# Clearing the padded buffers of a zipformer block early on VectorE, with a new instruction order

## The chip, the cores and the metric

The kernel runs on one core of one Trainium2 chip. The metric is the device time of one execution in microseconds (us). The engines are named as in the profile: PE is TensorE (PEld its weight loads), ACT is ScalarE, DVE is VectorE, POOL is GpSimd, and SP is SyncE, which here only issues DMAs.

## The reference

One block of a conformer-like speech encoder on x of shape (2, 4000, 144), in bfloat16, with 4 heads of 36:

```python
x = x + 0.5 * (silu(layernorm(x) @ w_ff1a) @ w_ff1b)
q, k, v = split(layernorm(x) @ w_qkv)              # 4 heads, Dh = 36
x = x + (softmax(q @ k.T * Dh**-0.5) @ v) @ w_o    # over all 4000 keys
a, b = halves(layernorm(x) @ w_pw1)
c = depthwise_conv5(a * sigmoid(b), dw)            # along time
x = x + silu(c) @ w_pw2
x = x + 0.5 * (silu(layernorm(x) @ w_ff2a) @ w_ff2b)
out = layernorm(x)
```

## The kernel before

**Work.** The 8000 rows are cut into 16 chunks of 500, eight for each of the two sequences; a chunk is four blocks of 125 rows. For each chunk `pre` does the first feed-forward part and the projections to Q, K and V; attention then goes over key tiles of 64 rows, four heads at a time; `post1` does the output projection and the gated unit, `post2` the convolution, the second feed-forward part and the last layer norm. Keys of a whole sequence must be there before its attention can end, so the first eight chunks go through `pre` in a set-up stage of some 70 us, in which the first attention tiles already run. All other chunks' work is mixed into the attention.

**Softmax.** TensorE writes a pair of score tiles to two PSUM banks. For most tiles ScalarE takes the exponential of 1000 columns in one instruction (PT from PS, 128x1000). For 190 tiles VectorE computes it with bit operations. TensorE then multiplies PT with V (VA).

**Layer norm and transposition.** `ln` (line 1068) takes statistics on VectorE (ST), the reciprocal root on GpSimd (RS), and the normalised rows XN, on VectorE for the first three chunks and in the tail, otherwise on GpSimd. The rows must then be transposed. In the calm case TensorE does that. Otherwise `blocks` (line 994) transposes 32x32 blocks in XN on VectorE, writes them in four DMAs to a DRAM scratch (`rows`), and reads them back with two DMAs as XT or XTQ, all on the SP queue, in order. The attention output AN goes the same way.

**The buffers that are cleared.** XN has 5 buffers of 640 columns, of which 576 hold data; AN has 4 of the same shape; XT has 5 buffers, whose second part (80 rows, 512 columns) holds 16 rows of data, while matmuls read all 80. The rest must be zero once, and so each buffer is cleared before its first use. All these clearings are GpSimd instructions: XN in `ln`, first 64 columns and later the whole buffer, XT in `transp` (line 1038), AN in `setup_dw` (line 930).

```python
op("pool", "memset", XNS[:, u, :] if inter else XNS[:, u, n * D:n * D + 64], 0.0, w=[("XN", u)], cost=0.56)
op("pool", "memset", XT[0:LP, s, 1, :, :], 0.0, w=wk, cost=0.5)
op("pool", "memset", ANS[:, :, :], 0.0, w=[("AN", a) for a in range(NAN)], cost=2.2)
```

**What sets the order.** A planner (`Sched` and the loop at the end of the kernel function) runs the generators and records every operation with `Rec.op`, from modelled costs. Operations recorded between two steps on one engine form a block. Then `Rec.reorder` (line 279) moves the blocks of every engine by the distances that the table `ORDER` (line 38) spells, one character each, and `PLACES` (line 111) names the PSUM bank of every tile. Waits are derived afterwards from the reads and writes of the recorded operations. Every engine works through its list strictly in order. All recorded instructions have one line in the profile, that of `replay`.

Of the kernel before, what the change touches and what calls it, by code (L numbers as in the profile page):

```python
# [12 lines left out]
D = 144  # L13
# [5 lines left out]
LP = 80  # L19
# [3 lines left out]
NB = 4  # L23
# [21 lines left out]
        "OOPNQNQOYP]CNNNNOMPMSO[NKOOQNVMPMMN`NbYMMMMNOMNIcLLNL[MMMNNQNRMJQLLROQSPLRNOQOPUQOMPQMPPRPVPLQOMQNPQ"
        "QQQSKPQSQKQQQQJPPPPPWQQSPKKQQUPPPSWPQRPQAVPPPQCVPQRPWHSYPHSOPQYPQEPQCPRZUPPSOOHDPR^OKOOOOPNOOOO^NOQN"
        "NOOOSNNNNS[NNNdRMNRKYNJWJNNNNNNGOOPP^YNNNNOMNNNNRNNPPPVROOLOOPPRZNNOOOOOPNOSOPNRPSMOOPQOQWNRPRLLNSZP"
        "NPQOIOQOTPPPRPQ]P^USPMMQIQKQQ8QTQQGMRRTQQKRRRRGLRSOMRPQQQJQQRPVP[OOOQEROO^IOQLNOOPPTTOMNQ[FOQNPPSPPM"
        "HPQOQQUPLOPNVPNOOSQNLUOOPNOXPPPLTQNLMPPPQOPPTOOPTPLOOQRNOPPPQOVPNOOOORZOP[PPMOOFRZOL[ROQKQTUBOKNFPPP"
        "_OOOOOOPNOOOOWNNVNNXMNTKMNOMZQOSLNOMSPSLLTPMOOUOPNOOTQOMOPPPQOPPPQOPPPTTQOSQSSSSNEEPQOPTPTMOMORSNNOP"  # L50
        "ROYPQOPQ^NPNPQOPAOOOOOSOOOPPPQQNPPPPPPXOOOOOOOaNPPPLOOOPUMOOOO[IOOPSOOQNPHPSWOOPPPPQGPPPPQQQMPPQQNPQ"
        "O_OOOPZOOOPI_NNNNZOPEOQWP^HKPHSJOLNOO`VPMRJOM^J`MPNKUNLUGNLJQNRIOPPRXOMOOOOPXMOPPMOOOPWOOPPPTKNOOPPP"
        "PPPPPPPQRPSYSQNQYZPRRRADIOXQGVOPJOORPIPPRRSSMR]MHOOQQQVRKNHPLPPPPPPPPPPRZQSQRRbHSGNQGPPQRRGLPQKQQQQJ"
        "QOQRPMQOPPQOSQNRMTROTNPXQQQEPJOQNPRPN_OPPPLRSOPLPPPGPPPSeOMPPQRJZPKLNNNN`NOKOVJNNNNcM`LMMMNNN]MNL]LL"
        "LLLLTWLXKMMVNQ_LMOPPQQ>MOOOTOMRbMMOOOOOTOOOQZIOPJMOOcOMPPT[PRORPEVHOPYCJQOQQGMOQQNQWNQNPPLSP_OaOOOPN"
        "PDPPPLOHPPQLPPPPQOTPNWNPPPWJNPPP`OIOPPPPPPPUQOELRP^TTQOZUPPCGOPQDJPPPPPPRPQWPRURPMFQQ_RPXDPQJLPNOJPN"
        "PPPPPSPPQ`PPTQQRERPQIQTNDPTPPJOPQQNPPUOPPSLPMPPRPQQRPJP[RNQQLaRJQSS[IQMGQQRPCZJPQOPQTPP@RPIPPPPQQQSS"
        "VXUQGNTQSSETDS`OQSCJQQdLOINQMRLLZMNSMMMMZLWPK]JMNLMTLNNNNVN`NNNNNROOPPJQOPLRPRMOQQRPLPXQQQRPTUQHFPQJ"
        "PPPPPPSPROUSPPTLPUOCOPNQOPROTWPRWRPVRZOY^YEOOPPMQ:;QDQQQQQQQQQEQQQMQOROVSMOTTQLVHROTRGNTVPHRPTRaJSQE"
        "QRSKNRNOQOPWQO=OOPNYOOOQNNOO]QOL_PNRO^NOUIPNK_MMW>MMMZMMMM]MMQLMMSNNOMOPPSOVNNPNXNPQOKQOQLQQQQUPPPHO"  # L60
        "QORPQMQOPQQSQOUVWNWMNOKOAOQOPPPPZWNNNOOLNNR^MNVNOMNNNNPSMN]NTNNNNNaNNNOQLN[RNOMRNHMSOSNPQGPQOPRXRPQW"
        "KOHOPPQYPPZPQRCO[I^NORFNNIZMMMNOWLNNNQMNRORRO_KPNOOOYNNNNNNOU^NSUHNKOJNOSOOQRJUPROTYMHNNURNNTMIPNQOU"
        "OOV[MNLNNNPYTNeJLNORNNGOO[]NNNNIQLMRLNRWOPUOO]OM`QO;LSOLO]JOJPRLLMRUNZMOVR[NPDOT^OOOFOSTOMNOSbPQLPRS"
        "_MORR_NPP^OHCNNNOZOWL~NHLMMNNNSOOXNOQQNSSOIVKPNPN]NOOOOOPPVOOOITNPPLPPQOWPPMRPNTKOOTNOPUMOOOQN`OOOPN"
        "OOPPPLOZOQQMPIQO^YROQQRLENO_PNPPPTQNNOROOSVO]QMNRNOPWTNOMNSOPQXbOOOQ[NO~NCdIMMMMMMMfbKMMMQMMJLMPLMUM"
        "MMNL^TR^JSLJQJUKPNLHQMPP`UNNNNOMOOOOPNOOPPPPQQNPQQQMUQQMSOPTQOPTPQUNQSPSQ<TRSSVEQQQHQQFPPPPPQSPMYTOL"
        "NNTMNNNP^[NOMNNQMMOLNN]PNOOR[OPKQN_ZLNESMOOKHOM[NPPLPNOOPPMQSTMNPQQQQRSQRRTCQVNGRNOMTTTMMNUPPQHNQSPM"
        "YVTQKLLSSOIJPSSPTMKORNOQOPPPPPPSORNSMRNRRRNQQRPFRPQQQQQQRPFQO"
    ),
    "act": (  # L70
        "PPPPPPPPPPPPPRSNNOSOOOPPPPPPPUPNOXNNOOOOOQNPPPPPPPPPROOPPQOPPPQOPPPPPPQQNPPPPPPPPPPPPPPPPPPPPPPPPPQO"
        "PPPPPPPPPPPPPPPPPPPPPPPPPPPPPPPPPPPPPPPPPPPPPPPPPPPPPPPPPPPPPPPPPPPPPPPPQOROSNOOPPPPPPPPPPPPPPPPPPPP"
        "PPPPPPPPPPPPPQOPPPPPPPPPPPPPPPPPPPPPPPPPQOPPQOPPPPPPPPPPPPPPPPPPPPPPPPPPPPPPPPPPPPPPPPPPPPPPPPPPPPPP"
        "PPPPPPPPPPPPPPPPPPPPPPPPPPPPPPPPPPPPPPPPPPPPPPPPPPPPPPPPPPPPPPPPPPPPPPPPPPPPPPPPPPPPPQOPPPPPPPPPPPPP"
        "PPPPPPPPPPPPPPPPPPPPPPPPPPPPPPQOPPQOPPPPPPPPPPPPPPPPPPPPPPPPPPPPPPPPPPPPPPPPPPPPROOPPQOPPPPPPPPPPPPP"
        "PPPPPPPPPPPPPPPPPPQOPPPPPPPPPPPPPPPPPPPPPPPPPQOQOPPPPPPPPPPPPPPPPPPPPPPPPPPPPPPPPPPPPPPPPPPPPPPPPPPP"
        "PPPPPPPPTOPNOPPPPPPPPPPPPPPPPPPPPPPPPPPPPPPPPPPPPPPPPPPPPPPPPPPPPPPPPPPQOPPPPQOPPPPPPPPPPPPPPPPPPPPP"
        "PPPPPPPPPPPPPPPPPPPPPPPPPPPPPPPPPPPPPPPROOPPQQNPPPPPPPPPPPPPPPPPPQOPPPPPPPQOPPPPPPPPPPPPPPPPPPPPPPPP"
        "PPPPPQOPPPPPPPPPPPPPPPPPROOPPPPPPPPPPPPPPPPPQOPPPPPPPPPPPPQOPPPPPPPPPPPPPPPPPPPPPPPPPPPPPPPPPPPPPPPP"
        "PQOPPPPPPPPPPPPQOPPPPPPPPPPPPPPPPPPPPPPPPPPPPPPPPPPPPPPPPPPPPPPPPPPPPPPPPPPQOPPPPPPPPPPPPPPPPPPPPPPP"  # L80
        "PPPPPPPPPPPPPPPPPPPPPPPPPPPPPPPPPQOSPNRNOQOUQNPMOPPPRORNQNPPPPPPQOROQQMPPPPPPQOPPPWORNNNOO"
    ),
# [2023 lines left out]
```

## Time and profile before

| | before |
|---|---|
| time, median of 3 runs (lowest to highest) | 881.2 us (880.84 to 882.3) |
| the profiled execution: span from first to last instruction | 880.5 us |
| the span against the median | 0.7 us below |
| instructions | 27000 |
| granted TensorE clock, mean | 0.998 |

The time of the profiled execution is known by its span; the other times are of executions without a profile. Windows are counted in us from the start of the span. In a row of the timeline the columns are the start, the duration, the engine, the operation with its tiles, and in brackets how long the engine was idle before it and what ended that. In a row of the groups they are the busy time and the mean duration in ns, then the idle time before the group. In a row of the windows they are the window, its length, the busy time of PE, PEld, DVE, ACT and POOL with the number of instructions, the clock, the share of the DMA engines and GB/s. A row of the waits has the total, the number of times and the longest. In the chain of work that ended last each row is a start, a duration and the engine and tile that it followed.

### The profile page before, as it was taken

The page shows a single profiled execution, that of the slowest core. Times are in us where ns is not written, and L with a number is a line of the kernel's source. Part 1 is how long each engine was busy: PE and PEld are TensorE (multiplying, and loading weights), DVE is VectorE, ACT ScalarE, POOL GpSimd, SP SyncE. Part 2 cuts the span into 40 slices and gives each one's busy share as a digit, 9 for nine tenths or more (in the row PEclk, how much of TensorE's full clock was granted, in tenths as well). Part 3 has the DMA queues.
Part 4 walks back from the last instruction along what each step waited for, and adds up shares of the span by engine and source line. Part 5 has one row for each costly group of instructions (what it writes and reads, how often), then busy time and mean ns, then how long its engine had stood idle before and what let it go on. Part 6 is the DMA issues. An engine that isn't in the chain of part 4 may idle for free.

```text
span 880.5 us, 27000 instructions
## 1 busy us (share of the span) xinstructions
PE 851.5 (97%) x11419; PEld 380.2 (43%) x11419; DVE 822.7 (93%) x1812; ACT 849.6 (96%) x1098; POOL 300.4 (34%) x584
## 2 busy tenths in 40 slices
PE   8998999999999999999999999999999999999996
PEld 6543433344444443443444444344443433444366
DVE  7977999999999999999989999899999999999987
ACT  6799999999999999999999999999999999999986
POOL 7770331431336130252111813522513404032434
PEclk9999999999999999999999999999999999999999
DMA  3221001220221110212001120110110011001111
GB/s 100 44 55 38 16 18 36 62 51 16 40 49 38 23 38 22 45 24 45 16 9 30 36 44 23 23 26 20 43 31 18 21 37 20 17 12 36 27 27 33
DMA packets 114351, 28.80 MB, mean 33 GB/s; under 512 B 101090, under 2 KB 114230, under 8 KB 114230
## 3 DMA queue, kind: packets, MB, share of 16 engines
q1 hardware_dynamic: 112646, 26.39, 13.8%
q8 instruction: 89, 1.46, 0.7%
q10 hardware_dynamic: 1584, 0.69, 0.3%
q14 instruction: 32, 0.26, 0.1%
HBM read 13.44 MB, written 13.61 MB: 31 GB/s over the span
## 4 chain that ended last, share of the span: by engine, by line
ACT 46%; PE 33%; DVE 17%; POOL 2%; DMA 1%; issue 1%; SPq 1%; POOLq 0%; DVEq 0%
ACT PT L398 42%; PE PS L398 33%; DVE PT L398 7%; ACT TH L398 4%; DVE HT L398 2%; DVE ST L398 2%; DVE X L398 2%; DVE XN L398 2%; POOL RS L398 1%; POOL XN L398 1%; DVE KT L398 1%; DVE QT L398 1%; DVE AN L398 1%; SPq L398 1%; DMA rows<-XN 0%
## 5 line engine op out<-in xcount | busy, mean ns | idle before, releaser
L398 ACT ACTIVATE PT<-PS 128x1000 bf16<-128x1000 f32 (+1 forms) x818 | 757.2, 1074 | 4.1 <-PE PS L398 2.4
L398 PE MATMUL PS<-QT,KT 64*64 64x500 bf16 x3968 | 425.7, 385 | 13.0 <-ACT PT L398 5.2
L398 PE MATMUL PS<-PT,VA 64*37 64x500 bf16 x4728 | 411.5, 372 | 1.8 <-DVE QT L398 0.7
L398 DVE TENSOR_SCALAR PT<-PS 128x500 int16<-128x500 f32 x380 | 250.1, 668 | 5.8 <-PE PS L398 3.9
L398 PEld LDWEIGHTS PS<-QT,KT 64*64 64x64 bf16 x3968 | 123.4, 104 | 236.8 <-ACT PT L398 137.1
L398 POOL TENSOR_SCALAR RS<-ST 125x4 f32<-125x4 f32 x130 | 37.0, 284 | 482.2 <-DVE ST L398 475.6
L398 PEld LDWEIGHTS PS<-PT,VA 64*37 64x37 bf16 x4728 | 141.4, 96 | 96.2 <-DVE PT L398 18.7
L398 DVE TENSOR_SCALAR PT<-PT 128x1000 uint16<-128x1000 uint16 x380 | 154.5, 418 | 2.1 <-PE PS L398 0.8
L398 POOL TENSOR_SCALAR XN<-X,RS 125x144 bf16<-125x144 bf16 x260 | 150.4, 610 | 13.1 <-DMA out_dram<-XN 6.4
L398 DVE TENSOR_TENSOR PT<-PT 128x1000 bf16<-128x1000 bf16 x190 | 128.8, 679 | 1.3
L398 ACT ACTIVATE TH<-PS 128x500 bf16<-128x500 f32 (+3 forms) x194 | 107.3, 575 | 7.4 <-PE PS L398 6.5
L398 POOL TENSOR_TENSOR RS<-RS,NHALF 125x4 f32<-125x4 f32 (+1 forms) x93 | 91.7, 989 | 33.1 <-DVE RS L398 27.3
L398 DVE SCALAR_TENSOR_TENSOR HT<-TH,PS 128x500 bf16<-128x500 bf16 (+1 forms) x135 | 81.2, 615 | 12.8 <-ACT TH L398 12.0
L398 PE MATMUL PS<-XT,WA 80*128 80x500 bf16 (+5 forms) x288 | 74.5, 365 | 2.2 <-DMA XT<-rows 0.9
L398 DVE BATCH_NORM_STATS2 ST<-X 125x6 f32<-125x288 bf16 x160 | 65.7, 447 | 2.8 <-DMA X<-in_x_dram 2.7
L398 DVE SCALAR_TENSOR_TENSOR X<-PS,X 125x288 bf16<-125x288 f32 (+1 forms) x128 | 56.6, 449 | 6.5 <-PE PS L398 5.2
L398 PE MATMUL PS<-WB,HT 128*125 128x144 bf16 (+1 forms) x640 | 52.4, 230 | 0.7 <-ACT HT L398 0.5
L398 PEld LDWEIGHTS PS<-WB,HT 128*125 128x125 bf16 (+1 forms) x640 | 44.3, 136 | 14.5 <-issue 3.8
L398 PEld LDWEIGHTS PS<-XT,WA 128*128 128x128 bf16 (+1 forms) x288 | 21.2, 97 | 38.8 <-issue 10.6
L398 PE MATMUL PS<-U,DG 128*128 128x250 bf16 (+6 forms) x204 | 29.6, 264 | 0.0
L398 DVE STREAM_TRANSPOSE XN<-XN 128x320 f32<-128x320 f32 x54 | 27.0, 500 | 1.0 <-POOL XN L398 1.0
L398 POOL COPY U<-U 128x2 bf16<-128x2 bf16 (+1 forms) x54 | 9.2, 209 | 46.3 <-DVE U L398 46.3
(95 smaller groups left out, 522.6 us busy)
## 6 DMA issues: line engine op xcount, KB each, us to landing
rows<-XN SPq DMA_DIRECT2D x216, 40.0 KB, 2.0
XT<-rows SPq DMA_DIRECT2D x56, 128.0 KB, 2.0
rows<-AN SPq DMA_DIRECT2D x60, 40.0 KB, 2.0
X<-in_x_dram SPq DMA_DIRECT2D x15, 140.6 KB
XTQ<-rows SPq DMA_DIRECT2D x26, 70.3 KB
out_dram<-XN SPq DMA_DIRECT2D x13, 140.6 KB
XT<-rows SPq DMA_DIRECT2D x56, 16.0 KB, 1.9
out_dram<-XN SPq DMA_DIRECT2D x3, 70.3 KB
```

The source lines that it names most:

```text
L398: ins = getattr(eng, o.name)(*o.a, **o.k)
```

## The change

The clearings of XN, XT and AN are recorded at the start, as 14 instructions on VectorE: five whole XN buffers, five XT parts, four AN buffers. They take no time in the planner, and their step numbers (a fraction of 1) make each a block of its own, so that `ORDER` can put it where it likes. Where GpSimd's clearings were recorded, a "ghost" is recorded, which keeps the planner's course; `reorder` takes the ghosts out and hands what they waited for on to what waited for them. `ORDER` and `PLACES` are new throughout (not shown). No other operation is added or taken away.

```diff
     def reorder(self, table):
+        real = {}
+
+        def through(o):
+            if id(o) not in real:
+                ds = {}
+                for d, raw in o.deps:
+                    for x, how in through(d) if d.ghost else [(d, raw)]:
+                        if x is not o:
+                            ds[id(x)] = (x, how or ds.get(id(x), (x, None))[1])
+                real[id(o)] = list(ds.values())
+            return real[id(o)]
+
+        for o in self.ops:
+            drop = o.shared - o.own
+            o.deps = [(d, raw) for d, raw in o.deps if id(d) not in drop]
+        for o in self.ops:
+            if any(d.ghost for d, raw in o.deps):
+                o.deps = through(o)
+        self.ops = [o for o in self.ops if not o.ghost]
...
+    def side(like, *a, **k):
+        kept = dict(R.free), R.kind, R.last, R.filling
+        R.filling = True
+        o = op(*a, cost=0.0, **k)
+        R.free, R.kind, R.last, R.filling = kept
...
+        return o
+
+    def early(j, what, w):
+        side(None, "dve", "memset", what, 0.0, w=w).step = j / 64
+
+    for u in range(NXN):
+        early(1 + u, XNS[:, u, :], [("XN", u)])
+    for s in range(NXT):
+        early(11 + s, XT[0:LP, s, 1, :, :], [("XT", s, i) for i in range(NB)])
+    for a in range(NAN):
+        early(21 + a, ANS[:, a, :], [("AN", a)])
...
     def setup_dw():
-        op("pool", "memset", ANS[:, :, :], 0.0, w=[("AN", a) for a in range(NAN)], cost=2.2)
+        op("pool", "ghost", w=[("AN", a) for a in range(NAN)], cost=2.2)
...
-            op("pool", "memset", XT[0:LP, s, 1, :, :], 0.0, w=wk, cost=0.5)
+            op("pool", "ghost", w=wk, cost=0.5)
...
-            op("pool", "memset", XNS[:, u, :] if inter else XNS[:, u, n * D:n * D + 64], 0.0, w=[("XN", u)], cost=0.56)
+            op("pool", "ghost", w=[("XN", u)], cost=0.56)
...
-            op("pool", "memset", XNS[:, u, :], 0.0, w=[("XN", u)], cost=0.0)
+            op("pool", "ghost", w=[("XN", u)], cost=0.0)
```

More of the change, by code (lines that the diff above doesn't have):

```diff
@@ L45 @@
[L45 to L54, printed above, removed]
@@ new lines @@
+        "NLMQLNOPSHcKMMOIbMMMMr^LLLLMZ]LNNOIDKkCKOLJRVSJKSKINVJRMMZDL^NKNNKOXLPLY[KZQJTLIGTKKKMPVTQMNLNTQOXOK"
+        "OOOOPUMOOOOSYNNNPYPNPNIOYOOPSYNNNOXOaOOTOOIRP^KPNRPNLPRPNPTRVT]PU[WP!F]P]CFKHKMNNNNPQLRPVPSOJNNPROZP"
+        "MOQQMPPPJROSQTUVOKNOPEPTOOOYTObNOVQOM[DGQMSMPUMKNDOQT[MN[MMVMMOMKNRKQMaOOOOVNNNXMOMQJM]UQOPPUQOYPRAL"
+        "Q@PMOPPQQNPPQOPTO]NNNOOOSNNNN^NOOPNQOWZKPLM]OPHOORPN[D`NLMNNW_LLLOUKILLOR`NIPLQOYOPNPNGNN]MO]WMMMMMM"
+        "NLMXNTVNVJLLQTLQHTPLVO[LNNN]Q`KMKYLLUKLLMKNKZQM^MN[ULMNLILMTMMPSKOOQTPMROZLPPSLOMPPQKPRP^PLQQMVLQNPP"
@@ new lines @@
+        "JQJTPWOZPPPPJFOOOQ]PPQOIPPPUOOOPUPPQOWAYOOOOJXOPRPWHRYNG^OPPWOODPPEOPJYOOSPMMNOO[PNOOOPNOOOOQfNOSNNN"
+        "NORNUMMVYMMM`YGLPXHLYURLJKKLS?NOQOSQ[NLPPMOQNNROMPPPTPPPLPPPPS[NNNPNQNPM`NNOOPN^QMMMOMOOLPNPQUL^VXLM"
+        "KLQLPK]ZOMOOQRN[URNK]OQOCOO6OQNNO[OO[NNNOOOPJSOOJROQRPUKOOPNTTZMMMMY`MMMQMM_IMMNNSOOWKIPYMKRNKWMOMNO"
+        "PNSQUMMOPNTPNOORPNQUNOPNO^QOPLUSPLOLJOQUMOSNNNTOWNNPMUNNNORNXNOOOOOOWNORNOMUN[]MN^YNOMIN[NCKMOFUMNaM"
+        "MMXNNZMMQLLZKKZLLRKM[RLJLMTR^_KLLINU^LLLNKMZIMNQMMVPKMNOOPXO^NNOMNNNRPNe^NPPQRPICKOMNWNVKMMMURLJNOQO"
@@ new lines @@
+        "NPPPPPPPTOPNOPPPPPPPPPPPPPPPPPPPPPPPPPPPPPPPPPQOPPPPPPPPPPPQOPPPPPPPPPPQOPPPPQOPPPPPPPPPPPPPPPPPPPPP"
+        "PPPPPQOPPPPPPPPQOPPPPPPPPPPPPPPPPPPPPPQRNOPPQQNPPPPPPPQQNPPPPPPPPPPPPPPPPPPPPPPPPPPPPPPPPPPPQOPPPQOP"
+        "PPPQOQOPPPPPPPPPPPPPPPPPPPPPPPPPPPPPPPPPPPPPPPPPPPPPPPPPPPQOPQOPPPPPPPPPPQOPPPPPPPPPPPPPPPPPPPPPPPPQ"
+        "OPQOPPPPPPPPPPQOPPPPPPPPPPQOPPPPPPPPPPPPPPPPPPPPPQOPPPPPPPPPPPPPPPPPPPPPPPPQOPPPPPPPPPQQQMPPPPPPPPPP"
+        "PPPPPPPPPPPPPPPPPPPPPPPPPPPPPPPPPPPRROQLRTNNSNRMNPPPPPSORNNRPRMQQMRORPMPPPPPPQOPPPWORNNNOO"
@@ new lines @@
+    "0245042504250235042504250425042504250425042504235023502430342035301430245320542042052504240524053205"
+    "2405420524052450240524052504250425042505240524052405240552404202304104130453140314210412041204131043"
+    "1034015301330510351035153010351304024302430243014301430243023501530243034203422034320540130134021402"
+    "1402140214021402140214143134021402140214021401340204131041304120431043104031430154301240124240204134"
+    "0134021402140210421041204120412041203422043024302431043023502420340503134020412042104214124021402140"
@@ new lines @@
+    "2140214013401340214020412040214012041204120412140214021402140204120402141124021402045240240525042052"
+    "4035052405240240120402342034203530120412040214020412041204120412412412014013402143425301503510351341"
+    "0430420342035320340134013402140120430253015301530153015301301035023510340134031530130104301430243014"
+    "1430243024302430243024302351030324032402340234013410431340135301530153015031503513513104321340134031"
+    "0431410420411043104301430135013403104310412043134013401204120412041204120412040214021424302350342024"
@@ L130 @@
+    "2034203420342034205303240234034034302430234023402430234023402405320525032040254103512350240524052054"
+    "2405250425042020420552045205420524042404220534052042505240524053202505423042305220440342034203420341"
+    "0340143024203420243024202430243024034202340243203500351530240224033503510351035103510530153010413412"
+    "0412041201412042041204024012412140214021403140214042304143042136542300505465042125443120135545404221"
+    "354123415354102430106312"
 )
@@ L145 @@
 class Op:
-    __slots__ = ("eng", "name", "a", "k", "idx", "deps", "clock", "inc", "waits", "cnt", "q", "done", "t0", "t1", "kind", "step", "tile", "shared", "own", "acc", "base")
+    __slots__ = ("eng", "name", "a", "k", "idx", "deps", "clock", "inc", "waits", "cnt", "q", "done", "t0", "t1", "kind", "step", "tile", "shared", "own", "acc", "base", "ghost")
 class Place(int):
@@ L868, in bass_standalone__conformer_family_zipformer__speech_kernel @@
     op("pool", "memset", WK[:, :, :, :], 0.0, w=["WK0"], cost=0.3)
+    def side(like, *a, **k):
[3 more added lines that the diff above has]
+        R.free, R.kind, R.last, R.filling = kept
+        if like is not None:
+            o.done = like.done
+        return o
[7 more added lines that the diff above has]
+        early(21 + a, ANS[:, a, :], [("AN", a)])
     def setup_v():
```

121 lines of the change are left out of this document (51 added, 70 removed).

## The prediction, made before the changed kernel ran

> **What bounds the kernel now.** I read the page's totals first, then the busy time by stage, then the waits, and last the chain of work that ended last.
>
> ```profile
> span 880.5 us, 27000 instructions
> PE 851.5 (97%) x11419; PEld 380.2 (43%) x11419; DVE 822.7 (93%) x1812; ACT 849.6 (96%) x1098; POOL 300.4 (34%) x584
> ...
> 0.00:20.00 20.00, 17.05 (x201) 14.48 (x201) 13.90 (x58) 11.93 (x27) 13.66 (x39) 1.00 0.43 108
> 20.00:46.00 26.00, 23.45 (x240) 13.02 (x240) 25.02 (x64) 20.15 (x37) 20.79 (x42) 1.00 0.20 40
> 46.00:55.00 9.00, 8.83 (x130) 4.44 (x126) 5.88 (x15) 9.00 (x12) 6.79 (x16) 1.00 0.31 59
> 55.00:75.00 20.00, 18.06 (x240) 6.62 (x242) 12.29 (x24) 18.25 (x25) 6.88 (x11) 1.00 0.28 63
> 75.00:100.00 25.00, 24.39 (x356) 10.75 (x354) 24.11 (x49) 24.90 (x30) 5.62 (x11) 1.00 0.03 11
> 100.00:840.00 740.00, 725.83 (x9869) 304.54 (x9872) 708.46 (x1495) 736.09 (x905) 230.35 (x438) 1.00 0.14 30
> 840.00:880.50 40.50, 33.85 (x398) 26.31 (x390) 33.08 (x114) 29.31 (x68) 16.35 (x31) 0.96 0.10 27
> ```
>
> The stage rows give PE, PEld, DVE, ACT and POOL busy in that order. Over the whole span ScalarE lacks 880.5 - 849.6 = 30.9 us of being always busy, and its work (the softmax exponentials and the tanh steps) is the same before and after. So the change can win only what ScalarE now stands idle, plus what its instructions lose by not following one another closely. By stage that idle time is 8.1 us (0 to 20), 5.9 (20 to 46), 0 (46 to 55), 1.8 (55 to 75), 0.1 (75 to 100), 3.9 (100 to 840) and 11.2 (840 to the end). From 20 to 46 us VectorE is the full engine (25.02 of 26), and GpSimd has much to do (20.79 of 26); from 46 on ScalarE is full. GpSimd, which does the clearings, is a third busy on the whole, so relieving it can matter only in the first 75 us.
>
> **The change, part by part.** GpSimd loses sixteen instructions: the large clearing of AN, five full and five small ones of XN, five of XT.
>
> ```profile
> L398 POOL MEMSET XN<- 128x640 bf16 x5 | 3.2, 630 | 0.0
> L398 POOL MEMSET XT<- 80x512 bf16 x5 | 2.6, 519 | 0.0
> L398 POOL MEMSET AN<- 128x2560 bf16 x1 | 2.2, 2227 | 0.0
> ...
> L398 DVE MEMSET WA<- 80x256 uint32 x1 | 0.3, 272 | 0.8 <-PEq L2091 0.8
> ...
> L398 DVE MEMSET KL<- 128x128 uint32 x1 | 0.2, 165 | 0.0
> ```
>
> The first three rows make 3.2 + 2.6 + 2.2 = 8.0 us off GpSimd; the five small ones come on top. VectorE gets fourteen clearings that are issued as 32-bit words: five of 320 words (XN), five of 256 (XT), four of 320 (AN). The last two rows give (272 - 165) / 128 = 0.84 ns a word, so 320 words take about 0.33 us and 256 take 0.27 (row WA): 9 x 0.33 + 5 x 0.27 = 4.3 us on VectorE. The counts of all other work agree between the two programs.
>
> *Term 1, the first 20 us.* VectorE has holes there.
>
> ```profile
> 3.91 0.46 DVE L398 BATCH_NORM_STATS2 ST<-X 125x6 f32<-125x288 bf16 x1 [2.09 <-DMA X<-in_x_dram]
> ...
> 5.47 0.54 DVE L398 TENSOR_SCALAR XN<-X,ST,RS 125x144 bf16<-125x144 bf16 x2
> ...
> 6.83 0.54 PE L398 MATMUL PS<-IDENT,XN 125*128 125x125 bf16 x4
> ...
> 8.03 0.27 DVE L398 MEMSET VA<- 128x248 bf16 x1 [0.83 <-issue]
> ```
>
> In the new order seven clearings (four XN, three XT) and two old ones (WPZ, DG) stand ahead of the first statistics instruction: 4 x 0.33 + 3 x 0.27 = 2.1 us plus 0.36 for the old two (176 and 120 words). The hole for the first x load is 2.09 us, so the first statistics start up to 0.4 us late; but WPZ and DG used to stand between the first and the second, so the second is on time. One XN and one AN clearing, 0.66 us, follow in the chain to the first XN, which moves from 5.47 to about 6.1 and ends at 6.7. Its reader is the transposition at 6.83, behind the 50 warm-up matmuls: just covered. The other five (three AN, two XT), 1.5 us, stand around the VA group, against its hole of 0.83 us and smaller ones until 11 us. Without that cover all 4.3 us would go to the path; with all of it, none. I take **+0.1 us** (0 to +1.2), nearest the two large holes.
>
> *Term 2, 20 to 46 us.* Here GpSimd's clearings stand in line ahead of the layer-norm work that feeds the transposing DMAs.
>
> ```profile
> 15.88 0.81 DVE L398 BATCH_NORM_STATS2 ST<-X 125x6 f32<-125x288 bf16 x2
> ...
> 17.32 0.20 POOL L398 TENSOR_SCALAR RS<-ST 125x4 f32<-125x4 f32 x1
> ...
> 19.11 1.94 POOL L398 TENSOR_SCALAR XN<-X,RS 125x144 bf16<-125x144 bf16 x4
> ...
> 19.32 0.68 DVE L398 CAST VA<-PS 128x504 bf16<-128x504 f32 x1
> ...
> 27.07 0.83 SPq L398 DMA_DIRECT2D XT<-rows  x2
> ...
> 31.54 1.52 PE L398 MATMUL PS<-XT,WA 128*128 128x500 bf16 x6
> ...
> 35.02 1.49 PEld L398 LDWEIGHTS PS<-XT,WA 128*128 128x128 bf16 x8 [1.37 <-DMA XT<-rows]
> ...
> 35.46 3.66 DVE L398 SCALAR_TENSOR_TENSOR HT<-TH,PS 128x500 bf16<-128x500 bf16 x7
> ```
>
> Without them the first such layer norm starts when its statistics end (15.88 + 0.81 = 16.69) and not at 17.32; with 0.1 us for the hand-over it ends about 0.55 us sooner (20.5 instead of 19.11 + 1.94 = 21.05), the second 0.63 + 0.52 more, or 1.7 us, the third 2.9. The 1.37 us for which TensorE's weight loads wait for XT go. But what is late next is VectorE: the HT row shows seven evictions back to back, and VectorE has only 26 - 25.02 = 1.0 us left in this stage. So the cap is 1.0, not 1.37. The change also adds a wait: VectorE's first block transposition now stands right behind the eviction of VA, at 19.32 + 0.68 = 20.0 us, and waits for GpSimd until 20.5; behind it, in order, stand the XN, XT and HT steps and thus TensorE. That costs up to 0.5. On the SP queue the second chunk's four writes now stand ahead of the first chunk's two reads of XT, so these start about 27.6 instead of 27.07 (four writes behind a second transposition that GpSimd allows from about 24.5); TensorE uses them from 31.54 on, so that is covered. I take **-0.6 us** (-1.0 to +1.0).
>
> *Term 3, 55 to 100 us.* This is the place where GpSimd's lateness reaches ScalarE.
>
> ```profile
> 59.62 2.23 POOL L398 MEMSET AN<- 128x2560 bf16 x1
> ...
> 65.33 3.64 DMA rows<-XN
> ...
> 70.27 2.57 DMA XTQ<-rows
> 72.88 0.96 PE PS L398 x6
> ...
> ACT PT L398 <- PE PS L398: 0.9, 3, 0.6
> ACT TH L398 <- PE PS L398: 0.7, 1, 0.7
> ```
>
> The three rows of the chain in the middle say that the set-up's last transposing DMAs end last at 65 to 73 us, and the wait rows (total, times, longest) that ScalarE stands for 1.6 us behind them. These DMAs start when GpSimd has written XN; it gets there earlier by the clearings of XN and XT still ahead of it, and AN's 2.23 us are gone as well. The DMAs should come about 2 us sooner, more than the 1.6 that ScalarE waits. I take **-1.5 us** (-1.85 to 0, the stage's whole idle time).
>
> *Term 4, 100 to 840 us.* No clearing is left here; only the new order and the new bank numbers act. Counted in the two instruction streams, TensorE's instructions that wait for a semaphore fall from 1846 to 1749, by 5.3%; changes between attention and other matmuls fall from 803 to 794. TensorE stands 740 - 725.8 = 14.2 us in this stage: 5.3% of it is 0.75 us. ScalarE loses more than its 3.9 idle us:
>
> ```profile
> 735.70 0.96 ACT TH L398 x2
> ...
> 781.83 26.51 ACT PT L398 x30
> ...
> L398 ACT ACTIVATE PT<-PS 128x1000 bf16<-128x1000 f32 x740 | 690.9, 1085 | 3.0 <-PE PS L398 1.5
> L398 ACT ACTIVATE TH<-PS 128x500 bf16<-128x500 f32 x104 | 68.4, 673 | 0.0
> ```
>
> Where exponentials follow closely, one takes 26.51 / 30 = 0.884 us, and a tanh 0.48. 740 x 0.884 + 104 x 0.48 = 704, and the smaller forms about 15: some 719 of 740 us. The 21 us between are starts that TensorE was late for. 5.3% of 21 is 1.1. That waits can be weighed by their number is a choice, not a finding. I take **-1.0 us** between ends at +4 (the visible idle time doubles) and -7 (a third of the 21 recovered).
>
> *Term 5, the end.* The instructions behind the last exponential are the same but for one tanh and one eviction that swap sides, and VectorE is full there. I take **0** (-1 to +1).
>
> The sum is 0.1 - 0.6 - 1.5 - 1.0 + 0 = -3.0 us, so a span of 877.5. The profiled span of 880.5 is 0.7 below the median of the runs shown, 881.2, so the predicted time is 877.5 + 0.7 = **878.2 us**.
>
> [...]
>
> **The rivals.**
>
> *No change that can be measured* (a measurement of this kernel tells about 0.2%, 1.8 us, from none): VectorE, not GpSimd, paces the set-up. For it: 25.02 of 26 us. Against it: the chain through the transposing DMAs at 65 us. Terms 2 and 3 would shrink to 0 and -0.5, term 4 to 0: 880.5 + 0.1 - 0.5 + 0.7 = 880.8 us. Chance 0.15.
>
> *Slower: TensorE's in-order queue in the long middle.* Every block was moved, and a PT x VA group placed ahead of the next scores while its exponential isn't ready holds up those scores, and so ScalarE.
>
> ```profile
> PEld PS L398 <- ACT PT L398: 148.3, 406, 1.1
> ```
>
> The price of one such event is the mean wait, 148.3 / 406 = 0.37 us, when the two score pairs in PSUM no longer cover it. It decides from where these waits outlive the cover: the gains of terms 1 to 3 are 2.0 us, so six more uncovered events bring the time back and 11 make it slower by more than 1.8. With 15 such events in 740 exponentials: 880.5 - 2.0 + 5.6 + 0.7 = 884.8 us. Against it: fewer waits in the stream. Chance 0.15.
>
> *Slower: the early clearings hold GpSimd up.* Its set-up clearings run beside VectorE's, and the reciprocal root of the first layer norm stands behind them.
>
> ```profile
> 1.36 0.46 DVE L398 MEMSET WB<- 64x72 uint32 x3
> ...
> 1.46 0.21 POOL L398 MEMSET WO<- 80x144 bf16 x1
> ...
> 3.21 0.21 POOL L398 MEMSET WB<- 64x144 bf16 x1
> ```
>
> If they excluded each other, the seven new ones would push that root by 2.1 us and with it the set-up: 878.2 + 2.1 + 0.6 = 880.9 us (the gain of term 2 lost too). Against it: 144 columns took 0.21 us both beside VectorE's clearing and alone. Chance 0.03, in with no change.
>
> *Much faster: a tighter middle.* If the new order takes a third of the 21 us, 878.2 - 6.0 = 872.2 us; with a sixth, 875.7. For it: fewer waits. Against it: VectorE has only 740 - 708.5 = 31.5 us free there, so it can't absorb much. Chance 0.12.
>
> That the clearings aren't moved at all is excluded: the instruction streams show fourteen on VectorE and none of XN, XT or AN on GpSimd.
>
> **How the numbers follow.** Forecast 0.55, much faster 0.12, no change 0.15, clearings that hold GpSimd up 0.03 (880.9 is no change either), slower 0.15. The forecast's bounds reach over 879.4, the line of 0.2% under the median, so 0.07 of its 0.55 count as no change. Faster by over 0.2%: 0.48 + 0.12 = 0.60; within 0.2%: 0.07 + 0.15 + 0.03 = 0.25; slower: 0.15. The range runs from 874.5 (about 0.07 of the much faster case left out) to 883.6 (about 0.10 of the slower case left out), so that some 0.17 is outside. The forecast's own range is 876.0 to 880.0.
>
> **What would show it right or wrong.** Term 1: the first VectorE statistics at 3.9 to 4.4 us and the first transposition of XN on TensorE still at 6.8 to 7.0. Term 2: no wait for XT by TensorE's weight loads near 35 us, VectorE at 25.5 or more of the 26 us to 46, ScalarE idle there for about 5.3. Term 3: ScalarE waits under 0.4 us between 55 and 100 us. Term 4: ScalarE idle for about 3 us from 100 to 840, and the mean of the 1000-wide exponentials under 1085 ns. The prediction is wrong if ScalarE's idle time in the set-up stays near 16 us, or grows in the middle beyond 6.

## The result, and the profile after

The changed kernel takes **885.4 us** (median of 5 runs, 884.3 to 887.9) against 881.2 us (880.8 to 882.9): 1.0048 of the time before, 95% interval 1.0033 to 1.0064. It is slower by 4.2 us where I forecast 3.0 us less, and outside the range of 874.5 to 883.6. Measured a second time, beside later experiments, it took 884.7 us against 881.7 (1.0039, 1.0024 to 1.0055). The ratios with their intervals are estimates of their own and need not equal the quotient of the medians. One execution of a later run, e8, showed a mean granted clock of 0.848 and 924.7 us and is left out everywhere.

The profiled execution of the changed kernel is its slowest, 887.9 us with a span of 886.1; so its 5.6 us above the span of before overstate the median's 4.2. In every run the time is 1.8 to 1.9 us above the span. The profiled execution of before, span 880.5, is one of 882.3 us, 1.1 above its median. The prediction took 0.7 us from span to time; that amounts to taking its 3.0 us off the median (881.2 - 3.0 = 878.2), so no part of the miss comes from it.

First the totals, then the same stages as in the prediction (PE, PEld, DVE, ACT, POOL busy, then the clock):

```profile
span 886.1 us, 27034 instructions
PE 850.9 (96%) x11419; PEld 382.4 (43%) x11419; DVE 825.6 (93%) x1826; ACT 850.3 (96%) x1098; POOL 289.8 (33%) x568
```

```profile
0.00:20.00 20.00, 15.83 (x162) 13.72 (x163) 16.25 (x67) 9.77 (x22) 11.74 (x31) 0.91 0.43 109
20.00:46.00 26.00, 24.43 (x260) 13.20 (x257) 24.96 (x64) 22.41 (x42) 16.17 (x33) 1.00 0.18 39
...
55.00:75.00 20.00, 18.39 (x237) 7.07 (x237) 12.38 (x23) 18.45 (x25) 4.91 (x11) 1.00 0.27 61
...
100.00:840.00 740.00, 720.81 (x9852) 305.27 (x9846) 703.78 (x1489) 732.65 (x902) 227.56 (x437) 1.00 0.14 30
```

ScalarE does the same work (850.3 us). It now stands idle for 10.2 us up to 20 us (before 8.1), 3.6 from 20 to 46 (5.9), 1.6 from 55 to 75 (1.8), 7.4 from 100 to 840 (3.9), and 12.8 behind that (11.2). The set-up as a whole is where it was; in this execution the loss is in the long middle and behind it. The experiments will show that the set-up's total hides a gain and a loss. Three places stand out.

**The first 20 us.** VectorE's timeline of the changed kernel, the clearings around the VA group:

```profile
7.58 0.33 DVE L419 MEMSET AN<- 128x320 uint32 x1
...
9.01 0.27 DVE L419 MEMSET VA<- 128x248 bf16 x1 [0.82 <-issue]
...
9.75 0.27 DVE L419 MEMSET XT<- 80x256 uint32 x1
10.04 0.66 DVE L419 MEMSET AN<- 128x320 uint32 x2
...
11.38 0.27 DVE L419 MEMSET XT<- 80x256 uint32 x1
...
13.83 0.54 DVE L419 TENSOR_SCALAR XN<-X,ST,RS 125x144 bf16<-125x144 bf16 x2
```

The hole of 0.83 us ahead of the VA clearing, which I counted as cover, is still there with 0.82: it moved with the instruction behind it, from 8.03 to 9.01, and took nothing in. The XN that Q and K are made from comes at 13.83 instead of 13.00, as the timeline of before has it:

```profile
13.00 0.54 DVE L398 TENSOR_SCALAR XN<-X,ST,RS 125x144 bf16<-125x144 bf16 x2
```

TensorE's timeline of the changed kernel, and its windows, cut where the granted clock changed at 15.77 and 19.18 us, show what follows:

```profile
14.43 0.41 PE L419 MATMUL PS<-IDENT,XN 125*72 125x125 bf16 x4 [1.40 <-DVE XN L419]
...
15.50 0.39 PE L419 MATMUL PS<-IDENT,XN 125*128 125x125 bf16 x4 [0.49 <-DVE XN L419]
```

```profile
12.35:15.77 3.42, 1.53 (x25) 1.19 (x23) 3.35 (x15) 1.21 (x3) 2.20 (x4) 1.00 0.54 136
15.77:19.18 3.41, 3.41 (x26) 2.83 (x24) 2.78 (x11) 1.60 (x5) 2.18 (x5) 0.50 0.41 98
```

Behind two holes of 1.40 and 0.49 us the granted clock is 0.50, for 3.41 us.

**Near 185 us.** The SP queue, a step of the chain, and TensorE:

```profile
176.60 1.95 SPq L419 DMA_DIRECT2D XT<-rows  x2
178.59 0.70 SPq L419 DMA_DIRECT2D X<-in_x_dram  x2
179.33 2.56 SPq L419 DMA_DIRECT2D rows<-AN  x4
181.94 1.09 SPq L419 DMA_DIRECT2D XT<-rows  x2
```

```profile
182.61 3.60 DMA XT<-rows
```

```profile
186.26 0.89 PE L419 MATMUL PS<-XT,WP 128*128 128x500 bf16 x2 [2.10 <-DMA XT<-rows]
```

SP issues one DMA after the other, with 0.04 to 0.05 us between these rows. The read of XT that TensorE needs stands behind four writes of AN, starts at 181.94 and lands 3.60 us after its second part; TensorE stands for 2.10 us, and a half clock follows (0.57 in the mean from 186 to 190). In the order of before this read stood ahead of the writes of AN:

```profile
179.79 0.83 SPq L398 DMA_DIRECT2D XT<-rows  x2
180.67 0.32 SPq L398 DMA_DIRECT2D X<-in_x_dram  x1
181.03 2.56 SPq L398 DMA_DIRECT2D rows<-AN  x4
```

**The end.** The last row of the chain that ended last, before and after, and the queue's last issues in the changed kernel:

```profile
876.71 0.23 DVEq L2076
```

```profile
880.86 0.23 DVEq L2116
```

```profile
879.51 1.28 SPq L419 DMA_DIRECT2D out_dram<-XN  x3
```

VectorE's part ends at 881.09, 5.0 us ahead of the span's end; before it was 876.94, 3.6 us ahead. Three of the last output writes are issued within 1.3 us, as one that waits for ScalarE stands ahead of a large one.

### The profile page after: what moved, and what is told of

The parts are those of the page before. It is cut to its first block, busy times and chain, and to the rows that moved or that the text cites. A ratio compares the mean times of both kernels' runs of the same rounds, so it can differ in the third digit from the quotient of the medians.

```text
span 886.1 us, 27034 instructions
## 1 busy us (share of the span) xinstructions
PE 850.9 (96%) x11419; PEld 382.4 (43%) x11419; DVE 825.6 (93%) x1826; ACT 850.3 (96%) x1098; POOL 289.8 (33%) x568
## 4 chain that ended last, share of the span: by engine, by line
ACT 40%; PE 31%; DVE 22%; POOL 2%; SPq 1%; DMA 1%; issue 1%; POOLq 0%; DVEq 0%
ACT PT L419 36%; PE PS L419 31%; DVE PT L419 10%; ACT TH L419 4%; DVE HT L419 2%; DVE ST L419 2%; DVE XN L419 2%; DVE X L419 2%; SPq L419 1%; POOL RS L419 1%; POOL XN L419 1%; DVE AN L419 1%; DMA XT<-rows 1%; DVE QT L419 1%; DVE KT L419 1%
## 5 line engine op out<-in xcount | busy, mean ns | idle before, releaser
L419 PE MATMUL PS<-PT,VA 64*37 64x500 bf16 x4728 | 406.4, 372 | 0.4 <-DVE QT L419 0.2
L419 PEld LDWEIGHTS PS<-QT,KT 64*64 64x64 bf16 x3968 | 126.2, 104 | 244.8 <-ACT PT L419 132.7
L419 POOL TENSOR_SCALAR XN<-X,RS 125x144 bf16<-125x144 bf16 x260 | 145.8, 590 | 8.3
L419 ACT ACTIVATE TH<-PS 128x500 bf16<-128x500 f32 (+3 forms) x194 | 103.6, 549 | 8.9 <-PE PS L419 7.4
L419 PE MATMUL PS<-XT,WA 128*128 128x500 bf16 (+4 forms) x288 | 75.0, 364 | 3.6 <-DMA XT<-rows 1.5
```

Of the source, the lines that this page charges most:

```text
L419: ins = getattr(eng, o.name)(*o.a, **o.k)
```

## The experiments

**Theory Q**: the loss is made at two places of SP's queue, near 185 us and at the end. **Theory S**: it is made by the clearings around the VA group, which delay the set-up. **Rival M**: the new order loses a little in many places. Medians; "before" is the kernel before on the same chip in the same series.

| run | us | before | ratio (95%) |
|---|---|---|---|
| e1 old order, clearings on VectorE | 883.55 | 881.37 | 1.0021 (1.0012 to 1.0030) |
| e2 changed, first swap | 884.29 | 881.37 | 1.0032 (1.0019 to 1.0044) |
| e3 changed, both swaps | 883.54 | 881.37 | 1.0027 (1.0015 to 1.0038) |
| e4 new order, clearings on GpSimd | 882.88 | 881.37 | 1.0016 (1.0004 to 1.0028) |
| e5 e3, six clearings moved | 881.33 | 881.81 | 0.9997 (0.9988 to 1.0005) |
| e6 e4, both swaps | 880.99 | 881.81 | 0.9988 (0.9980 to 0.9997) |
| e7 e1, six clearings moved | 881.42 | 881.81 | 0.9999 (0.9990 to 1.0008) |
| e8 e3, more warm-up matmuls | 882.11 | 881.81 | 1.0008 (1.0000 to 1.0017) |
| e9 e5, all in holes, warm-up | 882.51 | 881.66 | 1.0008 (0.9999 to 1.0016) |
| e10 the changed kernel again | 884.74 | 881.66 | 1.0039 (1.0024 to 1.0055) |
| e11 e9 without more warm-up | 881.46 | 881.81 | 1.0003 (0.9995 to 1.0012) |
| e12 e5 again | 881.75 | 881.81 | 1.0001 (0.9992 to 1.0010) |

### e1 and e4: one half of the change each

e1, VectorE's list in the order of before (banks of before too):

```diff
 WA, WB clearings
+XN2 XT0 XT3 XT4 XN4 XN3 XN1
 ST (first), RS, WPZ, DG, ST (second)
+XN0
 RS
+AN3
 XN, XN (first chunk)
+AN2
 KL, VL, VA clearings
+XT2 AN0 AN1
...
 ST
+XT1
 ST
```

> The order of the blocks and the banks are those of the kernel before; only the fourteen clearings go to VectorE, at the neighbours that they have in the changed kernel. Theory Q (the time is lost at two places of SP's queue that the new order made, one near 185 us, one at the very end): no change, 881.2 us, between 880.3 and 882.1. Theory S (the five clearings around the VA group delay the set-up and let TensorE's clock fall, and that is not regained): 881.2 + 2.2 = 883.4 us. Both expect the first XN for the Q tile late by about 0.8 us and a granted TensorE clock of 0.5 somewhere between 15 and 20 us.

e4, the code of the changed kernel with the clearings recorded on GpSimd again:

```diff
-    for u in range(NXN):
-        early(1 + u, XNS[:, u, :], [("XN", u)])
...
-            op("pool", "ghost", w=wk, cost=0.5)
+            op("pool", "memset", XT[0:LP, s, 1, :, :], 0.0, w=wk, cost=0.5)
```

> The changed kernel's order and banks, with the clearings back on GpSimd as in the kernel before (the small ones at its start, the full ones ahead of their layer norms, AN with U ahead of the tap block). Theory Q: both places of SP's queue are still there, so 885.4 us (884.3 to 886.3). Theory S: without the clearings on VectorE the first 20 us are those of the kernel before, 885.4 - 2.2 = 883.2 us.

Both came out as theory S said, at 883.55 and 882.88: each half costs, 2.2 and 1.5 us, and together about what the change costs. Theory Q alone falls. In e1's profiled execution the XN for Q was late by 0.4 us, not 0.8 (13.42), and the half clock that both theories expected did not come (clock 1.00 up to 20 us): that execution took 882.9. The mean granted clock of every execution is on record, and in e1 it parts two groups: the four executions with 0.998 or 0.999 took 882.0 to 882.9 us, the seven with 0.996 or 0.997 took 883.5 to 884.4. That fits a delay that always costs and a clock that falls in some executions only. It is a sign and not a measure, as this mean also holds a half clock at the end of the span (3.0 us of it in before, 3.3 in the changed kernel).

### e2 and e3: two swaps in SP's queue

```diff
 XT<-rows x2, X<-in_x_dram x2
-rows<-AN x4
 XT<-rows x2, X<-in_x_dram
+rows<-AN x4
...
-out_dram<-XN 125x288
 out_dram<-XN 125x576
+out_dram<-XN 125x288
 out_dram<-XN 1x288
```

> The changed kernel with two neighbouring blocks of SP's queue swapped, so that the reads of XT that TensorE waits for at 186.26 us stand ahead of the four writes of AN and not behind them, as in the kernel before. Theory Q: the reads issue about 179.4 and land about 181.5, before TensorE asks for them at 184.2; the wait of 2.1 us, the half clock of 3.4 us behind it and ScalarE's 3.4 us go: 885.4 - 3.4 = 882.0 us (881.3 to 882.8). Rival M (the new order loses a little in many places, and this wait is an accident of one execution): 884.9 or more.

> As the kernel with the swap near 185 us, and a second swap in SP's queue at the end: the write of the output that waits for nothing new is issued ahead of the one that waits for ScalarE. Theory Q: from the last exponential to the end 36.5 us where the changed kernel had 38.0, so another 1.4 us: 882.0 - 1.4 = 880.6 us (879.7 to 881.5). Rival M: less than 0.4 us for this swap, as the last write, issued behind VectorE's last step, sets the end: 882.0 if the first swap does what theory Q says, 884.9 if not.

Against before of its own series the changed kernel is at +4.2 us, and +3.1 when measured again (e10); e2 is at +2.9 and e3 at +2.2. So the first swap brought 0.2 to 1.3 us where theory Q expected 3.4, the second 0.7 of 1.4. Neither theory's number was met, and the intervals of e2 and e3 overlap, so the second swap by itself isn't clear of noise. The mechanism is as expected; SP's queue and TensorE in e2:

```profile
179.05 0.83 SPq L419 DMA_DIRECT2D XT<-rows  x2
...
180.28 2.55 SPq L419 DMA_DIRECT2D rows<-AN  x4
```

```profile
183.91 0.61 PE L419 MATMUL PS<-XT,WP 128*128 128x500 bf16 x2
```

The read starts 2.9 us sooner and TensorE doesn't wait, though only just: by the trace's semaphores the read lands at 183.54, 4.1 us after its second part (theory Q: about 181.5). In the kernel before it took 1.8 us from there, in e3 4.1 and in e5 3.9, always ahead of the writes; so the 3.60 us in the changed kernel aren't the price of the four writes ahead, but the late start is. The size that theory Q expected was read from one execution, the slowest. At the end, e3:

```profile
878.45 0.23 DVEq L2116
```

From there (878.68) to the end of its span of 882.4 it is 3.7 us, as before the change, where the changed kernel had 5.0.

### e10: the changed kernel again

> The changed kernel itself once more, unaltered, beside the run with everything in holes. Theory Q with theory S: the wait for XT near 185 us is there in this execution too (TensorE idle there for 1.5 to 2.2 us), as is the late first XN for the Q tile (13.7 to 13.9 us), and the time is 885.4 us (884.3 to 886.4). Whether the granted clock falls behind the two holes may differ from execution to execution: with both falls about 887, with none about 884. Rival A (the wait at 185 us was an accident of one execution): no wait over 0.5 us there, and 883.0 or less.

884.7 us, as theories Q and S said. The XN for Q is late again (13.84) and the holes behind it are the same, 1.40 and 0.49 us, but the clock stayed at 1.00, and near 185 us the hole is smaller:

```profile
10.22:13.64 3.42, 2.63 (x39) 2.26 (x37) 3.37 (x14) 2.55 (x5) 0.53 (x1) 1.00 0.68 159
13.64:17.05 3.41, 2.12 (x26) 1.72 (x27) 3.30 (x15) 1.27 (x4) 2.94 (x6) 1.00 0.45 120
17.05:20.46 3.41, 3.41 (x56) 2.35 (x53) 3.27 (x10) 3.24 (x10) 2.65 (x6) 1.00 0.29 59
```

```profile
184.38 0.62 PE L419 MATMUL PS<-XT,WP 128*128 128x500 bf16 x2 [0.77 <-DVE PT L419]
```

The hole of 0.77 us misses the 1.5 to 2.2 that I had expected; TensorE's weight loads waited 1.2 us for XT there. The same read at the same place landed 2.3 us after its second part, not 3.60. The two executions of one kernel differ by 886.1 - 882.9 = 3.2 us and by two half clocks of 3.41 us, at which TensorE loses 3.41 x (1 - 0.50) = 1.7 us each at most, by my estimate.

### e5, e6, e7: what is left when the faults are taken out

Six clearings moved (e5 in the new order, e7 in the old):

```diff
 RS
-AN3
 XN, XN (first chunk)
-AN2
 KL, VL, VA clearings
-XT2 AN0 AN1
 ST, ST
-XT1
+XT2 XT1
 ST
...
 VA<-PS
+AN0 AN1 AN2 AN3
 QT<-PS
```

> The changed kernel with both swaps in SP's queue, and with the six clearings that stood between the first layer norm's steps and around the VA group moved: the four of AN into VectorE's hole of 2.23 us near 66 us, two of XT behind the two statistics that end at about 9.5 us, where VectorE waits for x. Theory S (what is left, 883.5 against 881.4, is the delay of the set-up that these clearings make, with the half clock of TensorE behind it): the first XN for the Q tile moves from 13.8 to about 13.0 us, no half clock before 20 us, 883.5 - 2.0 = 881.5 us (880.6 to 882.3). Rival R (the rest of the new order, or the seven clearings ahead of the first statistics, cost it): 883.5 (882.7 to 884.3).

> The changed kernel's order and banks with the clearings on GpSimd, now with both swaps in SP's queue. By the terms measured so far they add up: 882.9 - 1.1 (the swap near 185 us) - 0.75 (the swap at the end) = 881.0 us (880.2 to 881.9). Rival R (the rest of the new order is dear as well): 882.4 or more.

> The order and banks of the kernel before with the clearings on VectorE, the six moved as in the run with the changed order. Theory S: the 2.2 us that the clearings cost in this order go, 881.4 us (880.6 to 882.2), and nothing is won, as the set-up's end does not hang on GpSimd. Rival R (the seven clearings ahead of the first statistics cost it): 883.0 or more.

All three were met: 881.33, 880.99, 881.42. In e5's timeline of VectorE the XN for Q is back at 12.88:

```profile
9.33 0.82 DVE L419 BATCH_NORM_STATS2 ST<-X 125x6 f32<-125x288 bf16 x2
10.15 0.55 DVE L419 MEMSET XT<- 80x256 uint32 x2
...
12.88 0.55 DVE L419 TENSOR_SCALAR XN<-X,ST,RS 125x144 bf16<-125x144 bf16 x2
```

The stages of e5, and then of e6, whose clearings are on GpSimd:

```profile
0.00:20.00 20.00, 16.07 (x201) 13.18 (x201) 17.20 (x68) 11.84 (x27) 13.10 (x34) 1.00 0.43 109
20.00:46.00 26.00, 23.86 (x240) 13.13 (x244) 24.58 (x64) 21.90 (x39) 16.27 (x33) 1.00 0.21 43
...
55.00:75.00 20.00, 19.08 (x252) 6.77 (x250) 14.54 (x28) 19.20 (x26) 3.51 (x8) 1.00 0.27 68
...
100.00:840.00 740.00, 722.78 (x9900) 306.93 (x9896) 706.72 (x1496) 735.81 (x905) 227.81 (x437) 1.00 0.14 30
```

```profile
0.00:20.00 20.00, 16.71 (x213) 13.55 (x213) 14.40 (x58) 12.68 (x29) 14.39 (x42) 1.00 0.43 110
20.00:46.00 26.00, 23.98 (x248) 13.08 (x240) 24.71 (x64) 21.50 (x38) 18.86 (x39) 1.00 0.22 44
...
55.00:75.00 20.00, 18.94 (x252) 6.74 (x244) 13.10 (x24) 19.39 (x25) 6.04 (x9) 1.00 0.28 69
```

In these three stages of the set-up ScalarE's idle time is 8.2 + 4.1 + 0.8 = 13.1 us in e5, and 7.3 + 4.5 + 0.6 = 12.4 in e6, against 15.7 before. Other executions show less: 14.1 in e12 (e5's kernel again), 13.9 in e4, and e7, with the old order, has 14.5. So with the clearings on VectorE the new order wins 0.4 to 1.4 us of idle time there (e12 and e5 against e7), with the clearings on GpSimd 1.8 to 3.2 (e4 and e6 against before), each from single executions. In the middle both have 4.1 to 4.2 us (100 to 840 of e6: 735.87 us busy), like before (3.9). e6 is the only version whose interval leaves out 1 on the faster side, and just so; it beats before by 0.8 us in the median, less than the 0.2% that I set as readable. The pair e4 and e6 gives both swaps a second time: +1.5 and -0.8 against before, so 2.3 us, and here the intervals don't overlap.

### e8: the clock by itself

```diff
-FILLS = (5, 2, 5, 12, 3, 1, 3) + (0,) * 60
+FILLS = (5, 2, 5, 26, 6, 1, 3) + (0,) * 60
```

> The changed kernel with both swaps, the clearings where they are, and 17 more warm-up matmuls on TensorE (14 and 3, of 0.056 us each) in its two holes at 13.0 and 15.0 us, which shrink from 1.40 and 0.49 to about 0.62 and 0.32 us. Theory C (it is the half clock that costs, not the late first XN): the granted clock stays 1.00 from 12 to 20 us, the first exponential starts about 1.5 us sooner than in the changed kernel, at 20.3, and the time is 883.5 - 1.3 = 882.2 us (881.4 to 882.8). Rival D (the delay of 0.85 us costs, and the half clock is regained by 46 us in any case): 883.5 (882.9 to 884.2).

882.11 us: theory C. The clearings are at their costly place, the XN for Q is as late, but TensorE's holes are filled:

```profile
14.44 0.41 PE L419 MATMUL PS<-IDENT,XN 125*72 125x125 bf16 x4 [0.62 <-DVE XN L419]
```

e3 is the same kernel with the holes, e5 the one without the delay as well. Against before of their series they are at +2.2 (e3), +0.3 (e8) and -0.5 us (e5): 1.9 for the clock and 0.8 for the delay (by the plain medians 1.4 and 0.8). The intervals of e3 and e8 just meet and those of e8 and e5 overlap, so the split is less sure than the whole. ScalarE's first exponential of 1000 columns shows the same split in the traces of before, of e8, and of the changed kernel:

```profile
19.29 1.04 ACT L398 ACTIVATE PT<-PS 128x1000 bf16<-128x1000 f32 x1
```

```profile
20.33 1.00 ACT L419 ACTIVATE PT<-PS 128x1000 bf16<-128x1000 f32 x1 [0.17 <-PE PS L419]
```

```profile
21.74 1.00 ACT L419 ACTIVATE PT<-PS 128x1000 bf16<-128x1000 f32 x1 [0.17 <-PE PS L419]
```

The late XN moves it by 1.0 us, the half clock by another 1.4; in e10, whose clock didn't fall, it starts at 20.33 too. So where the clock falls, more than half of what the six clearings cost is the clock.

### e9, e11, e12: everything in holes

e9 leaves six clearings ahead of the first statistics, puts WPZ and DG behind them again, XT4 with XT1 and XT2, AN near 66 us, and sets the two counts of FILLS to 20 and 6; e11 sets them back to 12 and 3; e12 is e5 once more.

> The changed order with both swaps in SP's queue, all fourteen clearings on VectorE, now only in its holes: six ahead of the first statistics (WPZ and DG again between the first and the second), one XN behind them, three XT where VectorE waits for x near 9.5 us, four AN near 66 us; and 8 and 3 more warm-up matmuls in TensorE's two holes at 13 and 15 us. Theory S (a clearing costs what it delays the chain to the first XN for the Q tile, nothing more): first statistics at 3.9 us, that XN at 12.9 to 13.0, no half clock, and 0.3 us under the run with six clearings moved: 881.0 us, 0.998 to 1.000 of the kernel before. Rival R (on GpSimd they are cheaper in any case, as VectorE is full up to 46 us): 881.6 or more, above the kernel before.

> The run with all fourteen clearings in holes, without its 11 more warm-up matmuls. That run was at 882.5 us in the median although its profiled execution (881.0) showed all that theory S expects of it. Theory F (the added matmuls cost in executions that were not profiled): 881.2 us (880.5 to 881.8). Theory P (three XT clearings and WPZ and DG at their new places cost): 882.5 (881.9 to 883.1). Neither, if it and the repeat of the run with six clearings moved agree with each other within 0.5 us.

> The run with both swaps and six clearings moved, once more and unaltered: 881.3 us by its first measurement (880.8 to 881.8), and 3.4 us under the changed kernel. If it comes out at 882 or more, the differences of 1 us between runs of different calls are not to be read, the one of the run with everything in holes among them.

e9 missed: 882.51 instead of 881.0, in the range of rival R, though its profiled execution (881.0 us, XN for Q at 12.95, clock 1.00 from 12 to 17 us) is what theory S says. e11, 881.46, and e12, 881.75, agree within 0.3 us. So the places of the clearings in e9 don't cost, and e9's 1 us is left to its 11 more matmuls or to chance; the intervals of e9 and e11 overlap, and this stays open. Rival R itself isn't excluded: with the clearings on GpSimd e6 is at -0.8, with them on VectorE e5, e11 and e12 are at -0.5, -0.4 and -0.1, and the intervals overlap. e12 and e5 are one kernel, and the clock is where their profiled executions part; e12, cut where its clock changed:

```profile
19.96:23.37 3.41, 1.91 (x22) 0.73 (x22) 2.39 (x8) 3.27 (x5) 2.87 (x7) 1.00 0.07 14
23.37:26.79 3.42, 3.42 (x20) 1.12 (x17) 2.99 (x8) 2.56 (x3) 2.95 (x6) 0.50 0.25 44
```

From 23.37 to 26.79 us e12's clock is 0.50; in e5 it is 1.00 there, behind the same holes. e12's span is 880.3, e5's 879.0: one half clock of 3.4 us goes with 1.3 us of the whole in this pair. In another pair, e11 with a mean clock of 0.996 and e9 with 0.997, the spans are 879.7 and 879.1, 0.6 us apart. In e5 and e12 TensorE is idle for up to 1.6 us in a stretch of 3.41 us there, in the kernel before for 1.0 at most.

## Why the prediction was wrong

The result is 7.2 us above the forecast. 3.0 of them are the gain that I had forecast (terms 2 to 4) and that hardly reaches the time. The other 4.2 are losses that the sum didn't hold: the clearings of term 1 that had no cover, and the SP queue, near 185 us (in the stage of term 4) and at the end (term 5).

**Term 1 (+0.1, 0 to +1.2): failed.** The failing step is "The other five (three AN and two XT) ... stand around the VA group, against its hole of 0.83 us and smaller ones until 11 us", with the value taken "nearest the two large holes". That hole is "issue", time in which VectorE waited for nothing that the profile shows, and it moved with the VA clearing. The five stood on the chain to the XN for Q, and so did the one of AN ahead of them. The clearings in all cost 2.2 us by e1; the six that were moved cost 2.3 to 2.7, e3's +2.2 against e5's -0.5 and e12's -0.1. More than half of that is the half clock where it comes, and no bound of mine held it. The signs that I named for this term gave no warning (first statistics at 4.34 us, first transposition of XN already at 6.51): they looked at the first XN, and the loss was at the next.

**Terms 2 and 3 (-0.6 and -1.5): the cause was wrong, and little of the gain reaches the time.** In term 2 the failing step is "Without them the first such layer norm starts when its statistics end", from which I let TensorE's wait of 1.37 us for XT go. The wait is gone in the changed kernel, but not because GpSimd is relieved. With GpSimd relieved and the old order it stays (1.37 us in e1, 1.36 in e7), and with the new order and the clearings on GpSimd it is gone too (e4, e6). From e7:

```profile
34.65 1.49 PEld L420 LDWEIGHTS PS<-XT,WA 128*128 128x128 bf16 x8 [1.36 <-DMA XT<-rows]
```

GpSimd does come earlier in e7, by 1.0 and 1.5 us for the second and third of these layer norms and not by 1.7 and 2.9, as each set of its XN took 2.3 us where it had taken 1.9. My cap of 1.0 us was wrong as well: from 20 to 46 us ScalarE's idle time fell by 1.8 us in e5 and by 1.4 in e6.

In term 3 the step "The DMAs should come about 2 us sooner" failed in the changed kernel. The read that its chain waits for ends at 70.9 us, where before's ended at 72.8:

```profile
67.84 3.04 DMA XT<-rows
...
70.93 0.64 PE PS L419 x2
```

But that is another read, XT in place of XTQ. The XTQ reads, the set-up's last, landed at 73.8 us, 0.9 later than before, since the set-up was late; TensorE no longer waited for them. ScalarE's idle time from 55 to 75 us stayed at 1.6. Without the delay the mechanism is there: in e7 these reads land at 70.7 us, 2.1 sooner, and ScalarE's idle time is 0.95 instead of 1.8. Yet e7's time gains nothing (0.9999). The new order with the clearings on GpSimd shortens the stage too (0.6 in e6). I worked the gain out along GpSimd's queue and never asked what a new order alone would give. In the median little of it arrives even in e5 and e12 (-0.5 and -0.1 us). The runs show two reasons: before's profiled execution, from which the gain is counted, was 1.1 us above its median, and behind the holes at 20 to 23 us a half clock came in e12 (0.50 from 23.37 to 26.79 us) and not in e5 (1.00).

**Term 4 (-1.0): failed.** Waits weighed by their number told nothing: with the faults out the stage has 4.1 to 4.2 us of idle time against 3.9. The mean of the 1000-wide exponentials fell from 1085 to 1065 ns, as I had asked for, in the changed kernel and in e5 alike:

```profile
L419 ACT ACTIVATE PT<-PS 128x1000 bf16<-128x1000 f32 x738 | 683.8, 1065 | 3.6 <-PE PS L419 3.0
```

ScalarE's busy time in the stage didn't fall with it (735.8 in e5, 736.1 before), and the same 740 exponentials fell into the stage. In the row above 738 x 1.065 = 786 us of instructions stand in 683.8 busy us: they overlap, and so their mean doesn't measure lost time, and the new order won nothing of the "21 us between"; whether any order could isn't shown. What came instead is one late read. Its mechanism was in none of my rivals: that the slower one gave 884.8 us, near the result, is luck, as it had matmuls out of turn on TensorE. I had followed the SP queue through the set-up only.

**Term 5 (0): failed by 1.4 us**, as I looked at VectorE's work and not at the writes behind it. The swap won back 0.7 us in the median.

By parts, each against before of its own series: the changed kernel at +4.2 or +3.1, with both swaps +2.2, with the six clearings moved as well -0.5 and -0.1, level with the kernel before. The two swaps are 0.9 to 2.0 us of the loss (2.3 with the clearings on GpSimd), the six clearings 2.3 to 2.7, and nothing else clear of noise is left. The rival in which early clearings hold GpSimd up didn't come: GpSimd's own clearings beside them took what they took before (0.21 us for 80x144, 0.53 for 80x512).

## What to carry to other kernels

A hole that the profile puts down to "issue" needn't be room for work (here it moved with its instruction and kept its 0.82 to 0.83 us), and a clearing counts where it stands on the way to the next tile that TensorE waits for, not where its engine has spare time (the XN for Q at 13.83 us, and at 12.88 with six clearings moved). When an order is new, follow every in-order DMA queue from end to end: one read behind four writes, and one waiting write ahead of a ready one, cost 0.9 to 2.0 us together here. Holes on TensorE had a second price behind them here, 3.41 us at a clock of 0.50 behind holes of 1.40 and 0.49 us, and as it came in one execution of the changed kernel and not in the next, one profile mustn't be used for its size. When a change brings a new order with it, run the new order without the change as well.

## What the runs showed of the hardware

Ahead of the end, a half clock lasted 3.41 or 3.42 us in the places shown here: 15.77 to 19.18 and 186.43 to 189.84 us in the changed kernel, 23.37 to 26.79 in e12 and 70.50 to 73.92 in e3. One more stands at the end of the span, 3.0 us of it in before (from 877.56) and 3.3 in the changed kernel (from 882.75), both without a matmul.

In the 3.4 us ahead of these falls TensorE was idle for 1.89 us (holes of 1.40 and 0.49) and 2.10 us (one hole) in the changed kernel, for 1.50 in e12 and for 1.01 in e3. The same does not always bring a fall: e10, the changed kernel again, has the same holes of 1.40 and 0.49 us and a clock of 1.00 behind them, and e5 has those of e12 and 1.00. So the same kernel pays in one execution and not in the next; what decides it isn't shown. The idle times rest on modelled ends of matmuls. The fall with the least idle time ahead of it, in e3:

```profile
67.09:70.50 3.41, 2.40 (x15) 0.76 (x16) 1.36 (x2) 3.16 (x4) 0.00 (x0) 1.00 0.29 66
70.50:73.92 3.42, 3.42 (x24) 1.12 (x26) 1.67 (x3) 2.17 (x3) 0.00 (x0) 0.50 0.26 70
```
